# Attention of chunks 4 to 23 with plain float32 score products on both row halves, in place of split q and k

## The chip, the cores and the metric

The kernel runs on one core of one Trainium2 chip. The metric is device time in microseconds (us) of one execution, as a median of several runs; lower is better. Engines are named as in the profile: PE is TensorE (PEld its weight loads), DVE is VectorE, ACT is ScalarE, POOL is GpSimd, SP is SyncE, which issues most transfers.

## The reference

Three parts follow one another, for 4 batches of 768 tokens (3072 tokens in all) and a model width of 512.

```
# 1. retention: 8 heads of width 64, decay gamma per head
state = gamma * state + k_t (outer) v_t
y_t   = scale * q_t @ state                       # q, k, v: (4, 8, 768, 64)
# 2. gated block, per token
xn = y / sqrt(mean(y*y) + 1e-6) * rms_g
x2 = (silu(xn @ w_gate) * (xn @ w_val)) @ w_out   # 512 -> 1536 -> 512
# 3. second block, per token
h = x2 @ w_in                                     # 512 -> 1024
u = h * softmax(h)
out = layernorm(u) * g_ln @ w_out2                # 1024 -> 512
```

The weights arrive as 64-bit floats. All results are wanted in float32 accuracy.

## The kernel before

**Precision.** The two feed-forward blocks use a fast float32 format (F32R in the code) whose operands carry fewer bits, so each operand is split in a high and a low part (`split`, L89: ACT copies the high part, DVE or POOL subtracts it). Each product then is three matmuls of 512 columns (`mm3`, L563: high·high, high·low, low·high, lines L564 to L566). Plain float32 matmuls appear in a trace as two records each.

**Tiling.** The tokens are worked on in six blocks of 512 (`NB`), each of four chunks of 128 tokens (`NCB`), 24 chunks in all; six chunks make a batch (`CPB`), at whose first chunk the retention state starts afresh (no product with the state) and at whose last none is kept. Within a chunk the recurrence is a small attention: scores k·q of 128 x 128 per head, times a decay mask (`mtab_t`), times v; plus the product of the decayed q (`qd`) with the state `U`; then `U` is decayed and the chunk's k·v (`kd`, decayed k) is added. A pair of heads (index p, halves hh) shares the 128 partitions: each head has 64 rows.

**Stages.** Chunks 0 to 3 are done in a prologue (`first_scores` and its neighbours). Then `bc_block(n)` runs the gated block of token block n: 12 steps (m), each with two groups of products into the PSUM banks GB and VB and one (`cmm`) into four banks X. `de_block(n)` runs the second block. Block 0's second block is held back and run after block 1's. While block n is being multiplied, the attention of block n+1 is fed in between: `att_pieces(n + 1)` returns a list of small functions that are spread over numbered slots (`span` slots; 30 for the attention of block 1, 45 for block 2, 35 for later ones), followed by the steps of the root-mean-square norm (`rms_steps`). In blocks 0 and 1 the weights are converted from 64-bit as well (`conv_a`, `conv_g`, `conv_b`, `w_split`, `w2_fin`): block 0 converts the gated block's weights and stores them split in DRAM, block 1 converts those of the second block (keys "in" and "out", 16 pieces). `conv_g` writes a sign tile: into the PSUM bank YB once the prologue is over, into the SBUF tile `sq` before that.

**Order of the work.** The tile framework orders the instructions of every engine by a simulated schedule with program order as priority; each engine and each transfer queue then works strictly in that order.

**Banks.** Of the eight PSUM banks, SB and YB serve attention. For each chunk before the change there are two units u of four heads, each with pieces a, b, c:
- Block 1 (chunks 4 to 7): `att_scores4`, four plain float32 products per unit on that unit's half of the rows (L195), one mask on DVE (L197).
- Blocks 2 to 5 (chunks 8 to 23): `att_prep` splits k and q (ACT L117 and L119, DVE L118 and L120): high k in one half of the rows and low k in the other, q high and q low side by side in 256 columns. `att_scores` then makes two heads' scores by two matmuls of 256 columns (L142); ACT copies the low-q half out (L146), DVE adds it (L148) and multiplies the mask (L149).
- `att_av` makes state·q (L159, full array) and A·v (L162, each head 64 columns of the array, so two heads stand side by side); `att_state` makes kd·v (L173, 64 columns too).

Of the kernel before, what the change touches and what calls it, by code (L numbers as in the profile page):

```python
# [35 lines left out]
ONE = (1, 2)  # L36
# [4 lines left out]
def retention_moe_kernel(ctx: ExitStack, tc: tile.TileContext, qk0, q2, kt, kv, wpk, w2i, w2o,  # L41
# [52 lines left out]
    raw, rawk = {}, {}  # L94

    def att_load(gc, u):
        tq = wt("rq", [P, 4, P], F32, 2)
        nc.sync.dma_start(tq, q2[gc, u])
        if u == 0:
            rawk[gc] = wt("rk", [P, 4, P], F32, 1)  # L100
            nc.sync.dma_start(rawk[gc], kt[gc])
        tv = wt("rv", [P, 512], F32, 2)
        nc.sync.dma_start(tv, kv[gc, u])
        raw[gc, u] = (tq, tv)

    prepd = {}

    def att_prep(gc, u, native=False):
        tq, tv = raw.pop((gc, u))
        tk = rawk[gc] if u == 0 else rawk.pop(gc)  # L110
        a, b = slice(64 * u, 64 * u + 64), slice(64 - 64 * u, 128 - 64 * u)
        if native:
            kst, qhl = tk[a], tq[a]
        else:
            kst = wt("kst", [P, 4, P], F32R, 2)
            qhl = wt("qhl", [P, 4, 2, P], F32R, 2)
            nc.scalar.copy(kst[a], tk[a])  # L117
            nc.vector.tensor_tensor(out=kst[b], in0=tk[a], in1=kst[a].bitcast(F32), op=ALU.subtract)  # L118
            nc.scalar.copy(qhl[:, :, 0, :], tq)  # L119
            nc.vector.tensor_tensor(out=qhl[:, :, 1, :], in0=tq, in1=qhl[:, :, 0, :].bitcast(F32), op=ALU.subtract)  # L120
        kd = qd = None
        if gc % CPB != CPB - 1:
            kd = wt("kd", [P, 4, 64], F32, 2)
            nc.gpsimd.tensor_tensor(
                out=kd, in0=tv[:, 0:256].rearrange("p (h d) -> p h d", h=4),
                in1=ktab_t[:, 4 * u:4 * u + 4].unsqueeze(2).to_broadcast([P, 4, 64]), op=ALU.mult)
        if gc % CPB != 0:
            qd = wt("qd", [P, 2, P], F32, 2)
            tq4 = tq.rearrange("p (a b) i -> p a b i", b=2)
            for hh in range(2):  # L130
                r = slice(64 * hh, 64 * hh + 64)
                nc.gpsimd.tensor_tensor(out=qd[r], in0=tq4[r, :, hh, :],  # L132
                                        in1=qtab_t[r, 2 * u:2 * u + 2, :], op=ALU.mult)
        prepd[gc, u] = (kst, qhl, kd, qd, tv)

    scored = {}

    def att_scores(gc, p):
        u, hl = p // 2, 2 * (p % 2)
        kst, qhl, kd, qd, tv = prepd[gc, u]  # L140
        for hh in range(2):
            nc.tensor.matmul(SB[:, hh * 256:hh * 256 + 256], lhsT=kst[:, hl + hh, :],  # L142
                             rhs=qhl[:, hl + hh].rearrange("p s i -> p (s i)"), start=True, stop=True)
        s4 = SB.rearrange("p (h s i) -> p h s i", h=2, s=2)
        s2 = wt("s2", [P, 2, P], F32, 1)
        nc.scalar.copy(s2, s4[:, :, 1, :])  # L146
        A = wt("A", [P, 2, P], F32, 2)
        nc.vector.tensor_tensor(out=A, in0=s4[:, :, 0, :], in1=s2, op=ALU.add)  # L148
        nc.vector.tensor_tensor(out=A, in0=A, in1=mtab_t[:, 2 * p:2 * p + 2, :], op=ALU.mult)  # L149
        scored[gc, p] = A  # L150

    def att_av(gc, p, Y=YB, at=0):
        u = p // 2
        kst, qhl, kd, qd, tv = prepd[gc, u]
        A = scored.pop((gc, p))
        cs = slice((p - at) * P, (p - at) * P + P)
        first = gc % CPB == 0
        if not first:
            nc.tensor.matmul(Y[:, cs], lhsT=U[gc % 2][:, p, :], rhs=qd[:, p % 2, :], start=True, stop=False)  # L159
        for hh in range(2):  # L160
            hl = 2 * (p % 2) + hh
            nc.tensor.matmul(Y[64 * hh:64 * hh + 64, cs], lhsT=tv[:, 256 + 64 * hl:320 + 64 * hl],  # L162
                             rhs=A[:, hh, :], start=first, stop=True)

    def att_state(gc, u, S=SB, at=0):
        if gc % CPB == CPB - 1:
            return
        kst, qhl, kd, qd, tv = prepd[gc, u]
        sv = S[:, at:at + 128].rearrange("p (a e) -> p a e", a=2)
        for pl in range(2):  # L170
            for hh in range(2):
                hl = 2 * pl + hh
                nc.tensor.matmul(sv[64 * hh:64 * hh + 64, pl, :], lhsT=kd[:, hl, :],  # L173
                                 rhs=tv[:, 256 + 64 * hl:320 + 64 * hl], start=True, stop=True)
        for hh in range(2):
            r = slice(64 * hh, 64 * hh + 64)
            ps = slice(2 * u, 2 * u + 2)
            state_update(gc, r, ps, sv[r])

    def state_update(gc, r, ps, sv):  # L180

        old, new = U[gc % 2][r, ps, r], U[(gc + 1) % 2][r, ps, r]
        if gc % CPB == 0:
            nc.vector.tensor_copy(new, sv)
        else:
            nc.gpsimd.tensor_tensor(out=new, in0=old,
                                    in1=utab_t[r, ps].unsqueeze(2).to_broadcast([64, ps.stop - ps.start, 64]),
                                    op=ALU.mult)
            nc.vector.tensor_tensor(out=new, in0=new, in1=sv, op=ALU.add)

    def att_scores4(gc, u, S=SB):

        kst, qhl, kd, qd, tv = prepd[gc, u]
        for hl in range(4):
            nc.tensor.matmul(S[:, hl * P:hl * P + P], lhsT=kst[:, hl, :], rhs=qhl[:, hl, :], start=True, stop=True)  # L195
        A = wt("r2", [P, 4, P], F32, 8)
        nc.vector.tensor_tensor(out=A, in0=S.rearrange("p (h i) -> p h i", h=4),  # L197
                                in1=mtab_t[:, 4 * u:4 * u + 4, :], op=ALU.mult)
        for pl in range(2):
            scored[gc, 2 * u + pl] = A[:, 2 * pl:2 * pl + 2, :]  # L200

    def att_y(gc, Y=YB):
# [7 lines left out]

    def att_yu(gc, u, Y):

        c = gc % NCB
        cs = slice(c * P, c * P + P)
        nc.scalar.copy(xT[:, 2 * u:2 * u + 2, cs], Y[:, 0:256].rearrange("p (a i) -> p a i", a=2))
        if u:
            sq = f4()[:, 0, :].rearrange("p (a i) -> p a i", a=4)
            nc.scalar.activation(sq, xT[:, :, cs], AF.Square)
            nc.vector.tensor_reduce(out=ssq[:, cs], in_=sq.rearrange("p a i -> p i a"), axis=AX.X, op=ALU.add)
# [95 lines left out]
    def first_scores(c, banks, halves=(0, 1)):  # L315

        for hh in halves:
            r = slice(64 * hh, 64 * hh + 64)
# [650 lines left out]
```

## Time and profile before

| | |
|---|---|
| median of 3 runs | 1041.49 us (1039.58, 1043.09, 1041.49) |
| the profiled execution | 1040.31 us, span 1038.5 us from its first to its last instruction |
| granted TensorE clock, mean | 0.995 of full speed |
| PE busy | 1014.7 us (98% of the span), 5174 matmul records |
| DVE, ACT, POOL busy | 542.5, 412.5, 329.5 us (52%, 40%, 32%) |

Busy times are unions of the intervals in which an engine's records run. Matmuls are pipelined and overlap, so what a matmul costs is read from the distance between the starts of its neighbours, not from its own duration.

### The profile page before, as it was taken

What the parts mean: (1) busy time and instruction counts of PE and PEld (TensorE: products, weight loads), DVE (VectorE), ACT (ScalarE), POOL (GpSimd) and SP (SyncE); (2) the same over time, 40 slices, a digit from 0 to 9 for tenths busy, and PEclk for the clock granted to TensorE, in tenths of its full rate; (3) what the DMA queues carried; (4) which work ended last, traced back from release to release, by engine and by line L of the source; (5) the groups of instructions that cost most, each with busy time, mean ns of one, the idle gap of its engine ahead of it and who ended that gap; (6) DMA issues with size and microseconds to landing.
All of it is one profiled execution on the core that took longest, in us unless ns stands there. A gap on an engine that the chain in (4) does not pass through costs nothing.

```text
span 1038.5 us, 14176 instructions
## 1 busy us (share of the span) xinstructions
PE 1014.7 (98%) x5174; PEld 817.8 (79%) x5174; DVE 542.5 (52%) x1014; ACT 412.5 (40%) x785; POOL 329.5 (32%) x414
## 2 busy tenths in 40 slices
PE   9899998998999999999999999999999999999998
PEld 7777876777888887878777877878787877888887
DVE  5887776787466733344681444483445366111162
ACT  3667655564345442222462322343223325211243
POOL 6876863675124221121251011142111015000031
PEclk9999998999999999999999999999999999999999
DMA  9699997796622015666403666510665510455301
GB/s 345 212 335 389 346 353 267 268 335 229 198 82 62 21 51 173 209 211 198 132 21 102 195 223 220 183 31 31 214 196 201 189 62 21 142 187 198 102 1 41
DMA packets 60485, 181.10 MB, mean 174 GB/s; under 512 B 7168, under 2 KB 7552, under 8 KB 60416
## 3 DMA queue, kind: packets, MB, share of 16 engines
q1 hardware_dynamic: 51632, 155.03, 44.6%
q10 hardware_dynamic: 8784, 25.17, 6.1%
q8 instruction: 41, 0.67, 0.3%
q14 instruction: 28, 0.23, 0.1%
HBM read 153.96 MB, written 26.21 MB: 173 GB/s over the span
## 4 chain that ended last, share of the span: by engine, by line
PE 80%; DVE 8%; issue 4%; POOL 4%; ACT 2%; DMA 1%; SPq 0%; ACTq 0%; POOLq 0%; DVEq 0%
PE X L565 11%; PE X L566 11%; PE X L564 11%; PE GB L564 7%; PE GB L566 7%; PE GB L565 7%; PE VB L564 6%; PE VB L566 6%; PE VB L565 6%; POOL st L470 2%; DVE st L469 1%; PE YB L162 1%; PE SB L142 1%; PE YB L159 1%; DVE st L482 1%
## 5 line engine op out<-in xcount | busy, mean ns | idle before, releaser
L581 DVE TENSOR_TENSOR f<-VB,f 128x512 f32<-128x512 f32 x72 | 49.6, 689 | 165.8 <-PE VB L566 156.9
L132 POOL TENSOR_TENSOR qd<-rq,qtab_t 64x256 f32<-64x256 f32 x68 | 56.3, 828 | 224.4 <-PE YB L159 145.7
L564 PE MATMUL GB<-xnh,w 128*128 128x512 f32 (+1 forms) x268 | 105.5, 394 | 1.2 <-ACT w L90 0.9
L564 PE MATMUL VB<-xnh,w 128*128 128x512 f32 (+1 forms) x268 | 106.0, 396 | 0.0
L565 PE MATMUL GB<-xnl,w 128*128 128x512 f32 (+1 forms) x268 | 104.7, 391 | 0.8 <-DVE xnl L286 0.8
L565 PE MATMUL X<-r,wo 128*128 128x512 f32 x264 | 104.3, 395 | 1.1 <-DVE r L91 1.1
L566 PE MATMUL GB<-xnh,w 128*128 128x512 f32 (+1 forms) x268 | 104.2, 389 | 0.3 <-DVE w L91 0.3
L566 PE MATMUL VB<-xnh,w 128*128 128x512 f32 (+1 forms) x268 | 104.2, 389 | 0.0
L565 PE MATMUL VB<-xnl,w 128*128 128x512 f32 (+1 forms) x268 | 103.8, 387 | 0.0
L566 PE MATMUL X<-r,wo 128*128 128x512 f32 x264 | 103.6, 392 | 0.0
L564 PE MATMUL X<-r,wo 128*128 128x512 f32 x264 | 98.2, 397 | 0.8 <-ACT r L90 0.8
L609 ACT ACTIVATE f<-GB 128x512 f32<-128x512 f32 x72 | 42.9, 596 | 134.8 <-PE GB L566 131.0
L90 ACT CAST r<-f 128x512 fp32r<-128x512 f32 x72 | 44.6, 619 | 113.3 <-DVE f L581 113.0
L470 POOL TENSOR_TENSOR st<-st,x 128x512 int32<-128x512 int32 x52 | 70.1, 1350 | 41.8 <-ACT x L467 14.1
L91 DVE TENSOR_TENSOR r<-f,r 128x512 fp32r<-128x512 f32 x72 | 59.6, 827 | 32.3 <-ACT r L90 32.0
L148 DVE TENSOR_TENSOR A<-SB,s 128x256 f32<-128x256 f32 x64 | 27.0, 422 | 91.4 <-ACT s L146 90.8
L681 POOL TENSOR_TENSOR sm<-sm 128x1 f32<-128x1 f32 x24 | 5.4, 225 | 201.2 <-DVE sm L659 170.3
L146 ACT COPY s<-SB 128x256 f32<-128x256 f32 x64 | 23.9, 374 | 98.6 <-PE SB L142 98.6
L564 PEld LDWEIGHTS GB<-xnh,w 128*128 128x128 f32 x268 | 50.5, 188 | 12.6 <-ACT w L90 1.4
L565 PEld LDWEIGHTS GB<-xnl,w 128*128 128x128 f32 x268 | 50.5, 188 | 11.4 <-DVE xnl L286 1.2
L564 PEld LDWEIGHTS VB<-xnh,w 128*128 128x128 f32 x268 | 50.5, 188 | 11.0 <-issue 1.2
L565 PEld LDWEIGHTS X<-r,wo 128*128 128x128 f32 x264 | 49.6, 188 | 11.9 <-DVE r L91 1.6
(241 smaller groups left out, 2358.1 us busy)
## 6 DMA issues: line engine op xcount, KB each, us to landing
w<-scr SPq DMA_DIRECT2D x120, 512.0 KB, 3.4
wo<-scr SPq DMA_DIRECT2D x60, 512.0 KB, 3.4
x<-in_wpk SPq DMA_DIRECT2D x36, 512.0 KB, 6.3
rq<-in_q SPq DMA_DIRECT2D x40, 256.0 KB, 3.5
rv<-in_kv SPq DMA_DIRECT2D x40, 256.0 KB, 3.5
scr<-CV ACTq DMA_DIRECT2D x18, 512.0 KB, 6.5
scr<-w ACTq DMA_DIRECT2D x12, 512.0 KB, 6.3
out<-f ACTq DMA_DIRECT2D x23, 256.0 KB, 2.0
```

Of the source, the lines that this page charges most:

```text
L90: nc.scalar.copy(hi, src)
L91: (lo_eng or nc.vector).tensor_tensor(out=lo, in0=src, in1=hi.bitcast(F32), op=ALU.subtract)
L132: nc.gpsimd.tensor_tensor(out=qd[r], in0=tq4[r, :, hh, :], in1=qtab_t[r, 2 * u:2 * u + 2, :], op=ALU.mult)
L142: nc.tensor.matmul(SB[:, hh * 256:hh * 256 + 256], lhsT=kst[:, hl + hh, :], rhs=qhl[:, hl + hh].rearrange("p s i -> p (s i)"), start=True, ...
L146: nc.scalar.copy(s2, s4[:, :, 1, :])
L148: nc.vector.tensor_tensor(out=A, in0=s4[:, :, 0, :], in1=s2, op=ALU.add)
L470: nc.gpsimd.tensor_tensor(out=ti, in0=ti, in1=lo, op=ALU.add)
L564: nc.tensor.matmul(ps, lhsT=lh, rhs=rh, start=start, stop=False)
L565: nc.tensor.matmul(ps, lhsT=lh, rhs=rl, start=False, stop=False)
L566: nc.tensor.matmul(ps, lhsT=ll, rhs=rh, start=False, stop=stop)
L581: nc.vector.tensor_tensor(out=a, in0=GV[1], in1=silu[:, 0, :], op=ALU.mult)
L609: nc.scalar.activation(s[:, 0, :], GV[0], AF.Silu)
```

## The change

The split of q and k goes. For chunks 4 to 23 a chunk is now one unit of eight heads. `att_load` brings q and k in pairs of heads (first head of a pair in rows 0 to 63, second in rows 64 to 127), by eight transfers of 64 KB, and k and v in one of 512 KB. `att_scores` makes plain float32 products of 128 columns, pair after pair and within a pair first the upper then the lower half of the rows, into SB and YB; each bank then gets one mask instruction (`att_mask`, 128x512). The pieces per chunk are: a (scores of all eight heads), b (state product, then preparation of the next chunk), c (state·q and A·v of all four pairs, evaluation, load of the chunk after the next). For block 1, where YB is in use by the conversion, the two halves' scores are separate pieces a0 and a1 through SB, then c, then d (state). `kd` and `qd` are one POOL instruction each per chunk. `conv_g` uses the SBUF tile `sq` for the 16 pieces of the second block's weights. `first_scores` of the prologue takes the two halves in turn too. At the start two whole chunks are loaded and one prepared, instead of two units and one.

```diff
-    def att_prep(gc, u, native=False):
...
-            kst = wt("kst", [P, 4, P], F32R, 2)
-            qhl = wt("qhl", [P, 4, 2, P], F32R, 2)
-            nc.scalar.copy(kst[a], tk[a])
-            nc.vector.tensor_tensor(out=kst[b], in0=tk[a], in1=kst[a].bitcast(F32), op=ALU.subtract)
-            nc.scalar.copy(qhl[:, :, 0, :], tq)
-            nc.vector.tensor_tensor(out=qhl[:, :, 1, :], in0=tq, in1=qhl[:, :, 0, :].bitcast(F32), op=ALU.subtract)
...
+    def att_load(gc):
+        tq, tk = wt("rq", [P, 4, P], F32, 2), wt("rk", [P, 4, P], F32, 2)
+        tv = wt("rv", [P, 2, 512], F32, 2)
+        for t, src in ((tk, lambda u: kt[gc, 64 * u:64 * u + 64]), (tq, lambda u: q2[gc, u, 0:64])):
+            for u in range(2):
+                heads = src(u).rearrange("d (a b i) -> d a b i", a=2, b=2)
+                for hh in range(2):
+                    nc.sync.dma_start(t[64 * hh:64 * hh + 64, 2 * u:2 * u + 2, :], heads[:, :, hh, :])
+        nc.sync.dma_start(tv, kv[gc].rearrange("u p x -> p u x"))
...
+    def att_mask(gc, hh, S):
+        A = wt("A", [P, 4, P], F32, 2)
+        nc.vector.tensor_tensor(out=A, in0=S.rearrange("p (a i) -> p a i", a=4), in1=mtab_t[:, hh::2, :], op=ALU.mult)
+        masked[gc, hh] = A
+
+    def att_scores(gc, halves, banks):
+        tq, tk = prepd[gc][0:2]
+        for p in range(4):
+            for hh in halves:
+                r = slice(64 * hh, 64 * hh + 64)
+                nc.tensor.matmul(banks[hh][:, p * P:p * P + P], lhsT=tk[r, p, :], rhs=tq[r, p, :],
+                                 start=True, stop=True)
+        for hh in halves:
+            att_mask(gc, hh, banks[hh])
...
+    def att_av(gc, Y):
...
+        for p in range(4):
+            cs = slice(p * P, p * P + P)
+            if not first:
+                nc.tensor.matmul(Y[:, cs], lhsT=U[gc % 2][:, p, :], rhs=qd[:, p, :], start=True, stop=False)
             for hh in range(2):
...
+                nc.tensor.matmul(Y[64 * hh:64 * hh + 64, cs], lhsT=att_v(tv, p, hh), rhs=A[hh][:, p, :],
+                                 start=first, stop=True)
...
     def first_scores(c, banks, halves=(0, 1)):
-        for hh in halves:
-            r = slice(64 * hh, 64 * hh + 64)
-            for p in range(4):
+        for p in range(4):
+            for hh in halves:
+                r = slice(64 * hh, 64 * hh + 64)
...
+            def a(gc=gc):
+                att_scores(gc, (0, 1), (SB, YB))
+            def a0(gc=gc):
+                att_scores(gc, (0,), (SB, SB))
+            def a1(gc=gc, nxt=nxt):
+                att_scores(gc, (1,), (SB, SB))
                 if nxt:
+                    att_prep(nxt)
+            def b(gc=gc, nxt=nxt):
+                att_state(gc, SB)
+                if nxt:
+                    att_prep(nxt)
+            def c(gc=gc, nx2=nx2, Y=SB if n == 1 else YB):
+                att_av(gc, Y)
+                att_y(gc, Y)
+                if nx2 and n > 1:
+                    att_load(nx2)
+            def d(gc=gc, nx2=nx2):
+                att_state(gc, SB)
                 if nx2:
+                    att_load(nx2)
+            out += [a0, a1, c, d] if n == 1 else [a, b, c]
...
     def conv_g(key):
-        g = YB if begun[0] else wt("sq", [P, 512], F32, 1)
+        g = YB if begun[0] and key[0] not in ("in", "out") else wt("sq", [P, 512], F32, 1)
...
-    att_load(NCB, 0)
-    att_load(NCB, 1)
-    att_prep(NCB, 0, native=True)
+    att_load(NCB)
+    att_load(NCB + 1)
+    att_prep(NCB)
```

## Rows read from the trace of the kernel before

**Rows 1.** The page, busy time by engine: us, share of span, instructions.

```profile
PE 1014.7 (98%) x5174; PEld 817.8 (79%) x5174; DVE 542.5 (52%) x1014; ACT 412.5 (40%) x785; POOL 329.5 (32%) x414
```

**Rows 2.** Stretches: length, busy PE, PEld, DVE, ACT, POOL (instructions), PEclk, DMA, GB/s.

```profile
34.00:60.00 26.00, 23.05 (x148) 18.12 (x146) 21.33 (x29) 14.46 (x25) 23.18 (x24) 1.00 0.64 200
...
150.00:166.00 16.00, 11.87 (x51) 8.35 (x51) 11.71 (x16) 10.22 (x18) 12.75 (x12) 0.94 0.98 373
166.00:172.00 6.00, 6.00 (x17) 4.84 (x18) 5.46 (x9) 4.77 (x9) 0.38 (x1) 0.59 0.73 260
172.00:289.00 117.00, 112.68 (x571) 90.30 (x570) 73.96 (x115) 56.64 (x104) 57.17 (x54) 1.00 0.73 248
...
383.00:505.00 122.00, 122.00 (x629) 97.44 (x628) 50.97 (x88) 36.03 (x68) 20.65 (x35) 1.00 0.59 195
505.00:526.00 21.00, 19.01 (x100) 15.03 (x99) 15.63 (x40) 8.57 (x20) 6.23 (x11) 1.00 0.16 46
526.00:532.00 6.00, 6.00 (x24) 4.83 (x23) 4.68 (x14) 1.82 (x5) 6.00 (x6) 0.72 0.01 3
...
690.00:698.00 8.00, 5.95 (x35) 4.78 (x33) 7.26 (x16) 7.40 (x17) 6.11 (x8) 1.00 0.00 0
```

**Rows 3.** Timeline of PE around a score pair and one A·v block.

```profile
423.86 0.40 PE L142 MATMUL SB<-qhl,kst 128*128 128x256 f32 x2
424.09 0.39 PE L566 MATMUL GB<-xnh,w 128*128 128x512 f32 x1
424.41 0.44 PE L162 MATMUL YB<-A,rv 128*64 128x128 f32 x4
...
425.12 0.39 PE L565 MATMUL GB<-xnl,w 128*128 128x512 f32 x1
425.35 0.39 PE L566 MATMUL GB<-xnh,w 128*128 128x512 f32 x1
```

**Rows 4.** Timeline of PE around a state product joined to an A·v.

```profile
429.25 0.39 PE L564 MATMUL X<-r,wo 128*128 128x512 f32 x1
429.57 0.45 PE L173 MATMUL SB<-rv,kd 128*64 128x64 f32 x8
429.85 0.39 PE L162 MATMUL YB<-A,rv 128*64 128x128 f32 x4
...
430.51 0.39 PE L566 MATMUL X<-r,wo 128*128 128x512 f32 x1
```

**Rows 5.** Timeline of PE around four plain float32 scores on one row half.

```profile
67.81 0.39 PE L565 MATMUL GB<-xnl,CV 128*128 128x512 f32 x1
68.13 1.16 PE L195 MATMUL SB<-rq,rk 64*128 64x128 f32 x8
...
69.55 0.39 PE L565 MATMUL VB<-xnl,CV 128*128 128x512 f32 x1
```

**Rows 6.** Timeline of PE, the prologue's scores of one chunk, one half after the other.

```profile
12.82 1.71 PE L320 MATMUL X<-QK 64*128 64x128 f32 x16
```

**Rows 7.** The conversion's last step (L482) by operand: ns min/median/max, first to last start.

```profile
L482 DVE SCALAR_TENSOR_TENSOR st<-st,YB x45: 670/676/690, 57.5 to 247.1; 128x512 f32<-128x512 f32 x45
...
L482 DVE SCALAR_TENSOR_TENSOR st<-st,sq x7: 673/683/1779, 21.8 to 53.6; 128x512 f32<-128x512 f32 x7
```

**Rows 8.** Groups on DVE, 165 to 289 us: busy us, mean ns | idle before.

```profile
L149 DVE TENSOR_TENSOR A<-A,mtab_t 128x256 f32<-128x256 f32 x12 | 8.8, 732 | 0.2
...
L120 DVE TENSOR_TENSOR qhl<-rq,qhl 128x512 fp32r<-128x512 f32 x6 | 5.5, 920 | 0.1
L118 DVE TENSOR_TENSOR kst<-rk,kst 64x512 fp32r<-64x512 f32 x6 | 5.2, 864 | 1.8 <-ACT kst L117 1.6
L148 DVE TENSOR_TENSOR A<-SB,s 128x256 f32<-128x256 f32 x12 | 5.0, 420 | 13.5 <-ACT s L146 13.4
```

**Rows 9.** The chain that ended last, 159 to 168 us: start, us, what.

```profile
160.32 0.68 DVE kst L118
...
163.54 0.69 DVE qhl L120
```

More of the change, by code (lines that the diff above doesn't have):

```diff
@@ L127, in att_prep @@
         if gc % CPB != 0:
-            qd = wt("qd", [P, 2, P], F32, 2)
-            tq4 = tq.rearrange("p (a b) i -> p a b i", b=2)
-            for hh in range(2):
-                r = slice(64 * hh, 64 * hh + 64)
[L132 to L163, printed above, removed]
@@ new lines, in att_v @@
+    def att_v(tv, p, hh):
+        h = 2 * p + hh
+        return tv[:, h // 4, 256 + 64 * (h % 4):320 + 64 * (h % 4)]
+    def att_av(gc, Y):
+        tq, tk, tv, kd, qd = prepd[gc]
+        first = gc % CPB == 0
+        A = [masked.pop((gc, hh)) for hh in range(2)]
+        for p in range(4):
+            cs = slice(p * P, p * P + P)
+            if not first:
+                nc.tensor.matmul(Y[:, cs], lhsT=U[gc % 2][:, p, :], rhs=qd[:, p, :], start=True, stop=False)
+            for hh in range(2):
+                nc.tensor.matmul(Y[64 * hh:64 * hh + 64, cs], lhsT=att_v(tv, p, hh), rhs=A[hh][:, p, :],
+                                 start=first, stop=True)
@@ L166, in att_state @@
+    def att_state(gc, S):
         if gc % CPB == CPB - 1:
             return
-        kst, qhl, kd, qd, tv = prepd[gc, u]
-        sv = S[:, at:at + 128].rearrange("p (a e) -> p a e", a=2)
-        for pl in range(2):
+        tq, tk, tv, kd, qd = prepd[gc]
+        sv = S[:, 0:256].rearrange("p (a e) -> p a e", a=4)
+        for p in range(4):
             for hh in range(2):
-                hl = 2 * pl + hh
-                nc.tensor.matmul(sv[64 * hh:64 * hh + 64, pl, :], lhsT=kd[:, hl, :],
-                                 rhs=tv[:, 256 + 64 * hl:320 + 64 * hl], start=True, stop=True)
+                h = 2 * p + hh
+                nc.tensor.matmul(sv[64 * hh:64 * hh + 64, p, :], lhsT=kd[:, h // 4, h % 4, :], rhs=att_v(tv, p, hh),
+                                 start=True, stop=True)
@@ L175, in att_state @@
         for hh in range(2):
             r = slice(64 * hh, 64 * hh + 64)
[L177 to L200, printed above, removed]
@@ L202, in att_y @@
-    def att_y(gc, Y=YB):
+            old, new = U[gc % 2][r, :, r], U[(gc + 1) % 2][r, :, r]
+            if gc % CPB == 0:
+                nc.vector.tensor_copy(new, sv[r])
+            else:
+                nc.gpsimd.tensor_tensor(out=new, in0=old, in1=utab_t[r].unsqueeze(2).to_broadcast([64, 4, 64]),
+                                        op=ALU.mult)
+                nc.vector.tensor_tensor(out=new, in0=new, in1=sv[r], op=ALU.add)
+    def att_y(gc, Y):
         c = gc % NCB
@@ new lines, in att_pieces @@
+        for gc in range(NCB * n, NCB * n + NCB):
+            nxt = gc + 1 if gc + 1 < NB * NCB else None
+            nx2 = gc + 2 if gc + 2 < NB * NCB else None
+            def a(gc=gc):
[4 more added lines that the diff above has]
+                att_scores(gc, (1,), (SB, SB))
+                if nxt:
+                    att_prep(nxt)
[10 more added lines that the diff above has]
+                att_state(gc, SB)
@@ L421, in c @@
                 if nx2:
-                    att_load(*nx2)
-            out += [a, b, c]
+                    att_load(nx2)
+            out += [a0, a1, c, d] if n == 1 else [a, b, c]
         return out
```

75 lines of the change are left out of this document (11 added, 64 removed).

## The prediction

> **What bounds the kernel now.** The page's first part comes first: PE runs 1014.7 of 1038.5 us, the next engine little over half [rows 1]. So what PE does in sequence is the time, and two things can change it: the length of PE's own work, and its gaps. The table of stretches says where the gaps are [rows 2]. From 383 to 505 us, where only attention and the first block run, PE is busy 122.00 of 122.00 us: whatever DVE and ACT save there is worth nothing, and whatever PE gets more is paid in full. Gaps stand in a few places: 2.95 us at 34 to 60, 4.1 at 150 to 166 (edge from block 0 to block 1), 4.3 at 172 to 289 (block 1, with the second conversion and attention of block 2), 2.0 at 505 to 526 (edge to block 3), 2.05 at 690 to 698. After two of them the granted clock drops: 0.59 on average over 166 to 172 and 0.72 over 526 to 532, which with levels of 1.2 and 2.4 GHz means 4.9 and 3.4 us at the lower one and half of that, 2.5 and 1.7 us, lost. After the gap at 690 it stays at 1.00 [rows 2].
>
> **What PE pays for attention.** Starts of neighbours give prices. An ordinary product takes 0.23 us (425.12 to 425.35), and a pair of heads' scores of split operands the same (423.86 to 424.09): 0.92 us a chunk [rows 3]. An A·v block in the middle of ordinary products costs far more than its work. From 424.09 to 425.12 is 1.03 us; less the two ordinary products in it, 0.57. Its four records run two by two (in 0.44 us with ends), 0.11 us each step, so 0.35 us is the price of going to 64-column halves and back [rows 3]. State and A·v together take 1.26 - 0.46 = 0.80 us, thus one such price, 0.22 for A·v and 0.23 for four state products [rows 4]. Four plain scores on one half of the rows take 1.74 - 0.46 = 1.28 us: eight records at 0.11 are 0.89, the way in and out 0.39 [rows 5].
>
> **The change on PE.** New scores of a chunk are sixteen records. If the halves overlap they take 0.89 + 0.39 = 1.28 us against 0.92. That they can overlap is seen in the prologue: eight on one half took 1.16 us [rows 5], so sixteen in a row would take 1.16 + 8 x 0.11 = 2.04; they took 1.71 though the second half is queued behind the whole first half [rows 6]. I take full overlap; without it a chunk costs 0.89 more.
> State is now a block of its own, 0.35 + 0.46 = 0.81; before, its two parts shared blocks with A·v and cost 0.23 each. A·v keeps four blocks a chunk, since state·q on the full array stands between the pairs in piece c; state·q itself is as often and as long. An ordinary chunk of blocks 2 to 5 thus goes from 0.92 + 2 x 0.57 + 2 x 0.80 = 3.66 to 1.28 + 0.81 + 4 x 0.57 = 4.37, +0.71 us; there are eleven. Chunks 11, 17 and 23 have no state: +0.36 each. Chunks 12 and 18 have no state·q, so the eight A·v share one block (0.35 + 0.88): 3.66 to 3.32, -0.34 each. Sum 7.8 + 1.1 - 0.7 = +8.2. In block 1 scores stay at two blocks of 1.28; chunks 4 and 7 give +0.35 each for the state's own block, 5 and 6 come out even: +0.7. Together +8.9 us, of which 25 more blocks are 25 x 0.35 = 8.8. Pieces that the schedule cuts in two pay the price again; I add 1.0 (three cuts), bounds 0 and 7 (one in each of 20 chunks).
> What the price consists of matters here. The row shows 0.09 us between the end of the ordinary step (424.09 + 0.23) and 424.41; the rest of 0.35 is weight loading that no longer hides and the way back [rows 3]. The Trainium skill (TensorEngine Tiling, Key Properties) says that changing the tiling mode drains the array, and speaks against a change with more changes of mode. Were the drain all, 25 blocks would cost 25 x 2 x 0.09 = 4.5 us instead of 8.8; I stay with the row.
>
> **What other engines lose, and what that frees.** For each unit ACT drops L117, L119 and two L146; DVE drops L118, L120 and two each of L148, L149. In 165 to 289 us these are 8.8 + 5.5 + 5.2 + 5.0 = 24.5 us of DVE [rows 8]. Eight masks of 128x512 with one operand in PSUM come in at some 0.68 (L482 in that form [rows 7]): 5.5 us. Against that, `conv_g` moves: the 16 conversions now read the sign tile from SBUF. With YB such an instruction takes 670 to 690 ns; with `sq` between 673 and 1779 [rows 7]. I take the middle of that range less 0.68, 0.55 each, 8.8 us (0 to 17.6). DVE in block 1 is left with 10.2 us less; in 172 to 289 it had 74 [rows 2].
> The gaps one by one. At 150 to 166 the chain runs through kst (0.68) and qhl (0.69) on DVE and a second kst between them, all ahead of what PE waits for [rows 9]: I take 2.6 of 4.1, and 2.5 for the clock, since a rest of 1.5 us is shorter than the gap at 690 that cost no clock. At 172 to 289 I take 4.0 of 4.3: A·v of block 2 waits for masks behind kst and qhl, and in the new order A is ready a whole piece before. At 505 to 526 DVE is busy 15.6 of 21 us with kst and qhl among it [rows 2]: 1.8 of 2.0, and 1.7 of clock. At 34 to 60 POOL is busy 23.2 of 26 us [rows 2], and preparation falls there from six instructions to two larger ones: 1.0 of 2.95. The gap at 690 I leave. In the prologue the interleaved scores are shorter by up to 0.55 us a chunk, mostly beside loads: 0.4 (0 to 2.2). Sum: 2.6 + 2.5 + 4.0 + 1.8 + 1.7 + 1.0 + 0.4 = 14.0; bounds 4 (only the prologue's and half of block 1's, the clock falls anyway) and 19.3 (all of it).
>
> **At no cost.** Nine transfers a chunk for five, with 1.02 MB for 1.28: each is asked for a whole chunk before its use, and DMA is at 0.59 in 383 to 505 [rows 2]. In block 0, where it stands at 0.98 around 150 us, small pieces could cost what the bytes save; without cover 0.5 MB of them at twice the time is 1.4 us a chunk at 373 GB/s, 5.6 in four. SP issues more, and weight loads queue behind; they have several slots in hand. Piece b waits on PE for the mask of SB, and c for that of YB; the pieces lie three slots apart and ordinary products fill them; if DVE is late, the next `cmm` is what waits. Fewer POOL instructions for kd and qd are idle time of an engine that seldom decides.
>
> **Sum.** 1040.31 + 8.9 + 1.0 - 14.0 = 1036.2 for an execution like the profiled one, which lies 1.2 us under the median of the runs; so 1037.4 as a median.
>
> **Rivals.** A measurement of this kernel tells 0.3%, 3.1 us, from no change: faster means below 1038.4, slower above 1044.6.
> First, the gaps shrink about as much as PE's work grows: relief of 7 to 12.5 us instead of 14.0, some 1041. For it: a schedule that is laid out anew often opens gaps elsewhere, and DVE at 690 is held up by the norm, not by attention.
> Second, the sign tile in SBUF keeps DVE the bottleneck of block 1: the conversion starts at the edge at 150 to 166 and lasts through block 1, so 2.6 + 2.5 + 4.0 = 9.1 us of relief hang on it: 1037.4 + 9.1 = 1046.5, slower. It decides when the 16 instructions take near 1.7 us each, so that 17.6 of the 19 us saved are gone. Against it: the median of the seven was 683 ns [rows 7]. The Trainium skill (SBUF — State Buffer, SBUF: two separate sides) says that a DVE instruction with two SBUF inputs and a GpSimd instruction lock each other out for a whole instruction; the 670 to 690 with YB and the 1779 with `sq` agree.
> Third, the halves of the rows do not overlap: 16 chunks x 0.89 = 14.2 more, 1051.6. The 1.71 us speak against it [rows 6].
> Fourth, everything is freed and no piece is cut: 1041.5 + 8.9 - 19.3 = 1031.1.
>
> **How the numbers follow.** Forecast with its neighbourhood up to the fourth case: 0.47 faster (0.37 and 0.10). First rival 0.29. Second 0.19, third 0.05. So faster 0.47, same 0.29, slower 0.24. The likeliest alone spans 1033 to 1038.4 or so; the range of 8 in 10 goes from 1030 to 1048, as it takes in the second rival and the fourth case and leaves out the third.
>
> **What would show it.** Right: score records of two halves that start within a few ns; 0.11 us steps; 1.28 us between the ordinary products around piece a; six blocks in an ordinary chunk; PE still gapless from 383 to 505 but that stretch longer by some 1.8 us (three times 0.71 less 0.34); no low clock after 166 and 526; L482 spread between 0.68 and 1.8. Wrong: gaps of over 2 us at the edges still there, or PE idle at piece a or b for a bank that DVE or ACT still reads, or pieces scattered in more blocks than six.

## The result, and the profile after

The changed kernel takes 1054.1 us in the median (1052.2 to 1055.8), against 1041.6 before: a ratio of 1.0121, 95% interval 1.0097 to 1.0145. That is slower by 12.5 us where 4 us faster was forecast. Of the 85 executions of the kernel before that were taken beside the runs below, 34 take 1049 to 1058 us with a mean granted clock of 0.97 to 0.98, where the others have 0.99 or more and a median of 1040.3 us; differences below are against 1040.3, and the ratios hold some of the former, which widens their intervals.

The page of the changed kernel, busy time by engine (us, share, instructions):

```profile
PE 1028.9 (98%) x5302; PEld 826.0 (79%) x5302; DVE 449.1 (43%) x822; ACT 354.1 (34%) x649; POOL 280.5 (27%) x321
```

The span is 1052.2 us, 13.7 more than before. PE's busy time rose by 14.2 us, while DVE lost 93 us and ACT 58 [rows 1]. PE's idle time is 23.3 us; before, it was 1038.5 - 1014.7 = 23.8. So PE does more, and the relief on the other engines bought no idle time back on balance. Where it went is in the stretches (columns as in [rows 2]; an edge is the passage from one block to the next):

```profile
0.00:34.00 34.00, 25.87 (x238) 20.95 (x238) 16.37 (x31) 12.57 (x28) 18.58 (x26) 0.87 0.83 284
34.00:60.00 26.00, 24.15 (x145) 20.30 (x146) 22.52 (x34) 16.46 (x29) 20.10 (x18) 0.84 0.75 252
...
150.00:164.00 14.00, 14.00 (x82) 11.36 (x81) 8.45 (x14) 7.19 (x13) 8.57 (x8) 1.00 1.02 410
164.00:172.00 8.00, 8.00 (x38) 6.04 (x37) 6.95 (x11) 4.84 (x9) 1.53 (x2) 1.00 0.69 268
172.00:289.00 117.00, 114.12 (x587) 89.49 (x585) 62.06 (x77) 45.70 (x77) 48.76 (x38) 1.00 0.72 243
...
383.00:508.00 125.00, 125.00 (x645) 99.38 (x643) 29.11 (x44) 24.87 (x42) 9.30 (x13) 1.00 0.55 177
...
526.00:532.00 6.00, 4.05 (x27) 3.16 (x26) 5.96 (x14) 1.98 (x4) 1.56 (x6) 0.87 0.19 54
...
690.00:706.00 16.00, 14.05 (x69) 11.09 (x68) 14.25 (x36) 7.18 (x16) 6.64 (x11) 0.89 0.12 34
...
857.00:878.00 21.00, 17.61 (x76) 14.17 (x75) 17.18 (x48) 8.63 (x20) 9.98 (x11) 0.92 0.00 1
```

The opening and the last edge before the change, in the same view:

```profile
0.00:34.00 34.00, 30.90 (x255) 24.71 (x256) 22.06 (x40) 16.35 (x35) 21.85 (x28) 1.00 0.89 322
...
855.00:875.00 20.00, 18.41 (x94) 15.07 (x93) 15.74 (x41) 10.94 (x23) 11.23 (x13) 1.00 0.04 14
```

Against these and [rows 2]: the gap of 4.1 us at 150 to 166 and the low clock behind it are gone, and block 1 idles 2.9 us instead of 4.3. But the gap in front of block 3 (1.95 us at 526 to 532) and that at 690 to 706 are as large as before, the one at 857 to 878 has 3.4 us for 1.6, the clock drops behind all three, and the opening up to 34 us idles 8.1 us for 3.1.

The same view from the first ordinary product (a product of the feed-forward blocks) to the end, the changed kernel first:

```profile
37.49:1052.18 1014.69, 1000.47 (x5055) 802.86 (x5055) 429.23 (x785) 338.09 (x615) 260.04 (x293) 0.99 0.49 163
34.47:1038.52 1004.05, 983.30 (x4918) 792.78 (x4917) 520.00 (x975) 396.09 (x750) 307.25 (x386) 0.99 0.50 169
```

The first product comes 3.0 us later, and the rest takes 10.7 us more. Of these, idle time is -6.5 (14.2 for 20.75). The half clock takes 7.5 us of the busy time (it lasts up to 42.3 us, and for 3.4 us at each of the three edges) where it took 2.5 + 1.7 = 4.2: +3.3. What is left, PE's own work at full clock, is 993.0 for 979.1: +13.9.

A chunk's scores on PE's timeline, in the middle of block 2's attention:

```profile
450.84 0.39 PE L510 MATMUL VB<-xnh,w 128*128 128x512 f32 x1
451.16 0.37 PE L129 MATMUL SB<-rq,rk 64*128 64x128 f32 x1
451.17 0.37 PE L129 MATMUL YB<-rq,rk 64*128 64x128 f32 x1
451.37 0.27 PE L129 MATMUL SB<-rq,rk 64*128 64x128 f32 x1
451.38 0.27 PE L129 MATMUL YB<-rq,rk 64*128 64x128 f32 x1
451.48 0.27 PE L129 MATMUL SB<-rq,rk 64*128 64x128 f32 x1
...
452.25 0.50 PE L508 MATMUL X<-r,wo 128*128 128x512 f32 x1
```

The halves overlap: records come in pairs 6 to 7 ns apart, one of each half, in steps of 0.11 us after a first of 0.21. From 450.84 + 0.23 to 452.25 is 1.18 us where 1.28 was reckoned. What was not reckoned stands a little earlier:

```profile
389.45 0.39 PE L510 MATMUL GB<-xnh,w 128*128 128x512 f32 x1
389.77 0.43 PE L147 MATMUL YB<-A,rv 128*64 128x128 f32 x2
390.13 0.48 PE L129 MATMUL SB<-rq,rk 64*128 64x128 f32 x2
390.55 0.50 PE L508 MATMUL X<-w2oh,r 128*128 128x512 f32 x1
390.89 0.40 PE L509 MATMUL X<-w2ol,r 128*128 128x512 f32 x1
391.21 0.48 PE L129 MATMUL SB<-rq,rk 64*128 64x128 f32 x2
391.63 0.50 PE L510 MATMUL X<-w2oh,r 128*128 128x512 f32 x1
```

A plain float32 product leaves two records. So this is one product of A and v, one score, two ordinary products and again one score: the schedule has drawn products of several pieces ahead, one at a time. Each pays the way off the full array and back: from 389.45 + 0.23 to 390.55, 0.87 us for two products of 0.22; from 390.89 + 0.23 to 391.63, 0.51 for one. Call a group a run of neighbouring records on one division of the array (half its rows or half its columns), and count from 45 us on: there were 87 before and are 135 now, 48 more where 25 were reckoned.

The theory after the result: the loss is the number of groups, at 0.35 us each as in [rows 3]; beside it stand an opening delayed by small transfers, and gaps at the edges that have another cause than the attention's work on DVE. The rivals: grouping costs nothing (drawn-ahead products fill waits), or one cause carries it all.

### The profile page after: what moved, and what is told of

Its sections match the earlier page's. It is cut to its first block, busy times and chain, and to the rows that moved or that the text cites. A ratio compares the mean times of both kernels' runs of the same rounds, so it can differ in the third digit from the quotient of the medians.

```text
span 1052.2 us, 13974 instructions
## 1 busy us (share of the span) xinstructions
PE 1028.9 (98%) x5302; PEld 826.0 (79%) x5302; DVE 449.1 (43%) x822; ACT 354.1 (34%) x649; POOL 280.5 (27%) x321
## 4 chain that ended last, share of the span: by engine, by line
PE 89%; DVE 6%; DMA 3%; POOL 1%; issue 1%; ACT 1%; SPq 0%; POOLq 0%; ACTq 0%; DVEq 0%
PE X L508 11%; PE X L510 11%; PE X L509 11%; PE GB L508 8%; PE GB L509 8%; PE GB L510 8%; PE VB L508 7%; PE VB L510 7%; PE VB L509 7%; PE YB L147 2%; PE SB L129 2%; PE YB L145 2%; DVE st L426 2%; PE X L616 1%; PE SB L158 1%; DMA x<-in_wpk 1%
## 5 line engine op out<-in xcount | busy, mean ns | idle before, releaser
L90 DVE TENSOR_TENSOR r<-f,r 128x512 fp32r<-128x512 f32 x72 | 54.8, 762 | 36.3 <-ACT r L89 35.8
L166 POOL TENSOR_TENSOR U<-U,utab_t 64x256 f32<-64x256 f32 x26 | 18.4, 707 | 191.6 <-PE YB L145 190.1
L508 PEld LDWEIGHTS VB<-xnh,w 128*128 128x128 f32 x268 | 50.4, 188 | 15.4 <-DVE f L525 3.7
L508 PEld LDWEIGHTS GB<-xnh,w 128*128 128x128 f32 x268 | 50.8, 190 | 11.2 <-ACT xnh L240 0.5
L509 PEld LDWEIGHTS GB<-xnl,w 128*128 128x128 f32 x268 | 50.8, 190 | 10.7 <-DVE xnl L244 0.8
L510 PEld LDWEIGHTS GB<-xnh,w 128*128 128x128 f32 x268 | 50.8, 189 | 10.1
L510 PEld LDWEIGHTS VB<-xnh,w 128*128 128x128 f32 x268 | 50.4, 188 | 10.5 <-issue 0.2
L509 PEld LDWEIGHTS VB<-xnl,w 128*128 128x128 f32 x268 | 50.4, 188 | 9.8
```

Of the source, the lines that this page charges most:

```text
L90: (lo_eng or nc.vector).tensor_tensor(out=lo, in0=src, in1=hi.bitcast(F32), op=ALU.subtract)
L508: nc.tensor.matmul(ps, lhsT=lh, rhs=rh, start=start, stop=False)
L509: nc.tensor.matmul(ps, lhsT=lh, rhs=rl, start=False, stop=False)
L510: nc.tensor.matmul(ps, lhsT=ll, rhs=rh, start=False, stop=stop)
```

## Experiments

### The number of groups

`uncut`: the attention's products are queued behind the last ordinary product traced before them.

```diff
+    lastmm = [None]
...
+    def behind():
+        return tc.issue_after(lastmm[0].ins) if lastmm[0] else nullcontext()
...
-        nc.tensor.matmul(ps, lhsT=ll, rhs=rh, start=False, stop=stop)
+        lastmm[0] = nc.tensor.matmul(ps, lhsT=ll, rhs=rh, start=False, stop=stop)
...
-                att_av(gc, Y)
+                with behind():
+                    att_av(gc, Y)
```

The same stands around the scores and the state's products.

> The attention's products of chunks 4 to 23 may no longer be drawn ahead of the last ordinary product traced before them, so that a group of a piece stays together in TensorE's order; the built order then has 118 groups of products off the full array after the first ordinary product, against 137 in the changed kernel. Theory (a group of products off the full array costs about 0.36 us, and the change made 48 more such groups, not 25): 19 groups fewer, -7 us, 1047 us. Rival A (a drawn-ahead product filled a wait, so that keeping the groups together only brings the waits back): 1054 us with the waits on TensorE up by 7 us. Rival B (the loss lies in the small transfers at the start and in the low clock, not in the groups): 1054 us.

`ufirst`: the four state products of a chunk ahead of its eight products of A and v.

```diff
+        for p in range(0 if first else 4):
+            cs = slice(p * P, p * P + P)
+            nc.tensor.matmul(Y[:, cs], lhsT=U[gc % 2][:, p, :], rhs=qd[:, p, :], start=p == 0, stop=False)
         for p in range(4):
             cs = slice(p * P, p * P + P)
-            if not first:
-                nc.tensor.matmul(Y[:, cs], lhsT=U[gc % 2][:, p, :], rhs=qd[:, p, :], start=True, stop=False)
             for hh in range(2):
...
-                                 start=first, stop=True)
+                                 start=first, stop=first or p == 3)
```

> In piece c the four state products (full array) are issued first and the eight products of A and v behind them, in one group instead of four; the work is the same. The built order has 89 groups off the full array, against 137 in the changed kernel. Theory (a group costs about 0.36 us): 48 groups fewer, -17 us, 1037 us. Rival A (the products of A and v cost what they cost, however they are grouped): 1054 us. Rival B (the small transfers at the start and the low clock carry the loss): 1054 us, all of TensorE's records off the ordinary products unchanged in sum.

`both`: the two edits together.

> Both edits together, the groups kept whole and the state products first: 67 groups off the full array against 137. Theory: 70 fewer at 0.36 us, -25 us, 1029 us. Rival A: waits come back for the drawn-ahead products, some 1035 to 1040 us. Rival B: 1054 us.

`merge`: as `both`, and in blocks 2 to 5 the state's products move from piece b to behind A·v in piece c (the edit against `both`).

```diff
             def b(gc=gc, nxt=nxt):
-                with behind():
-                    att_state(gc, SB)
...
                 with behind():
                     att_av(gc, Y)
+                    if Y is YB:
+                        att_state(gc, SB)
```

> As before it, and in blocks 2 to 5 the products of the state's update stand directly behind those of A and v, so that a chunk has two groups off the full array: 54 in all against 137. Theory: 83 fewer at 0.36 us, -30 us, 1024 us, if nothing waits for the later state. Rival A: the state comes too late for the next chunk and TensorE waits some 0.5 us for it in each of 16 chunks, 1030 us or more. Rival B: 1054 us.

Measured (groups counted in the records after 45 us; the changed kernel and the four made from it have the same 5302 records on PE):

| kernel | median us | ratio to before, interval | groups | PE busy us |
|---|---|---|---|---|
| before | 1040.3 | | 87 | 1014.7 |
| changed | 1054.1 | 1.0121 (1.0097 to 1.0145) | 135 | 1028.9 |
| uncut | 1048.0 | 1.0055 (1.0021 to 1.0090) | 117 | 1024.0 |
| ufirst | 1039.3 | 0.9967 (0.9933 to 1.0001) | 87 | 1012.9 |
| both | 1031.8 | 0.9909 (0.9879 to 0.9938) | 66 | 1002.4 |
| merge | 1025.3 | 0.9854 (0.9806 to 0.9902) | 53 | 995.3 |

The times lie within 3 us of what the theory gave. By the medians a group costs (1054.1 - 1025.3) / 82 = 0.35 us, by the busy time (1028.9 - 995.3) / 82 = 0.41. The clock doesn't carry this: PE's work behind the first ordinary product, without idle time and with the half clock taken out as above, falls from 993.0 to 962.1 us, 0.37 a group. The first rival falls: less than 5 us of waits came back (idle 27.8 us in `merge`, 23.3 in the changed kernel). With before's 87 groups (`ufirst`) the change is worth 1 us, which cannot be told from nothing. One chunk of `ufirst` on PE's timeline:

```profile
465.19 0.39 PE L511 MATMUL VB<-xnh,w 128*128 128x512 f32 x1
465.41 1.05 PE L144 MATMUL YB<-qd,U 128*128 128x128 f32 x8
466.40 1.09 PE L148 MATMUL YB<-A,rv 128*64 128x128 f32 x16
467.42 0.50 PE L509 MATMUL X<-r,wo 128*128 128x512 f32 x1
```

State·q and A·v of a whole chunk take 2.0 us here, from 465.42 to 467.42; in four groups of 0.57 [rows 3] A·v alone took 2.3. The Trainium skill (TensorEngine Tiling, Key Properties) says that a change of the tiling mode drains the array. The ranking by groups agrees; the 0.09 us that [rows 3] show on the way in, taken for both ways, would be 0.18 a group, and 0.35 was measured.

### The opening

On the changed kernel's timeline of SP, ACT and PE, nine transfers for chunk 4 and then chunk 5's stand in SP's order, the latter around a load of weights (x):

```profile
15.57 4.48 SPq L102 DMA_DIRECT2D rk<-in_kt  x4
20.09 4.28 SPq L102 DMA_DIRECT2D rq<-in_q  x4
24.41 0.59 SPq L103 DMA_DIRECT2D rv<-in_kv  x1
25.05 3.29 SPq L102 DMA_DIRECT2D rk<-in_kt  x4
28.38 0.61 SPq L102 DMA_DIRECT2D rq<-in_q  x1
29.12 0.50 SPq L389 DMA_DIRECT2D x<-in_wpk  x1
...
25.21 1.13 ACT L207 ACTIVATE xT<-YB,rg_t 128x128 f32<-128x128 f32 x4
...
31.26 0.75 ACT L411 ACTIVATE x<-x,two 128x512 f32<-128x512 uint32 x1 [4.93 <-DMA rk<-in_kt]
...
34.14 2.08 PE L710 MATMUL SB<-f,ones 128*128 128x128 f32 x8 [4.71 <-ACT f L205]
```

ACT idles 4.9 us ahead of L411, and the work for the next chunk's norm (L205) is queued behind it; PE waits 4.7 us for that, and runs at half clock from 32.1 to 42.3 us. The first ordinary product comes at 37.5 us, before at 34.5.

It is not the weights that ACT waits for, though the expectations below take it so. The piece of x that L411 reads (by the semaphore that it waits for, 104 in the trace) was issued at 14.29 us and had landed at 23.82. The chain that ended last, 22 to 38 us (start, us, what), names what released ACT:

```profile
26.27 4.52 DMA rk<-in_kt
...
30.82 0.02 ACTq L457
...
30.87 0.34 ACTq L457
31.26 0.75 ACT x L411
```

L457 is ACT's own store of converted weights (scr<-w), which stands ahead of L411 in ACT's order. In the trace it carries the same semaphore (108) as a transfer of chunk 5's k that was issued at 26.27, and it waits until that one has landed, at 30.80. So an engine that reads nothing of chunk 5 stands behind one of its transfers. The runs below move or merge these transfers, and both ways of the delay, a late load of weights and a store behind a transfer, would go with that; it is the trace that tells them apart.

`start1`: the second chunk's `att_load` moves from the start into block 1's first piece.

> The loads of the second chunk after the opening (chunk 5: eight transfers of 64 KB and one of 512 KB) are issued in the first piece of block 1's attention instead of at the start. Theory (the first ordinary product is late because SP issues these transfers in front of a load of expert weights, and TensorE idles 5.0 us at 29.1 us and runs at half clock behind it): the first product comes at 35 us instead of 37.5, the whole takes 3 us less, 1051 us. Rival (the load that is late would be late anyway, for the first chunk's eight transfers or for the queue's bytes): 1054 us with the first product at 37.5 us.

1054.7 us, ratio 1.0086 (1.0040 to 1.0133): nothing. The schedule put the transfers into the same place of SP's order, so the run tells of neither. `start3` queues them behind a later load on SP:

```diff
-        nc.sync.dma_start(t, src)
+        lastx[0] = nc.sync.dma_start(t, src)
...
+                if gc == NCB:
+                    with tc.issue_after(lastx[0].ins):
+                        att_load(nxt)
...
-    att_load(NCB + 1)
```

> The loads of chunk 5 (eight of 64 KB, one of 512 KB) are held on SP behind later loads of expert weights, so that SP's order has them eight places later. (The earlier edit start1 left SP's order as it was, so it tested nothing.) Theory (these transfers stand in front of the weights for which ScalarE, and behind it TensorE, waits 5.0 us at 29.1 us): the weight load is issued some 7 us sooner, at 25 us or before, the wait falls to under 1 us as in the kernel before, first ordinary product near 34.5 us against 37.5, -3 us, 1051 us. Rival (the wait stays because the first chunk's eight transfers alone hold SP up to 24 us): 1053 to 1054 us.

1053.2 us, ratio 1.0134 (1.0099 to 1.0169). The first ordinary product came at 34.4 us, as the theory said, and the end did not follow: the chunk was late in its turn. PE waited 1.4 us up to 79 us, and 1.8 us up to 169, the edge to block 1, and by the 480th ordinary product the kernel was 4.5 us behind the changed one.

`bigload`: q and k of a chunk side by side in the input.

```diff
...
-                for hh in range(2):
-                    nc.sync.dma_start(t[64 * hh:64 * hh + 64, 2 * u:2 * u + 2, :], heads[:, :, hh, :])
...
+        t = wt("rqk", [P, 2, 4, P], F32, 2)
...
+        nc.sync.dma_start(t, q2[gc])
```

> q and k of a chunk lie side by side in the input, as the array's rows take them, so that a chunk's loads are two transfers of 512 KB instead of eight of 64 KB and one of 512 KB; nothing else changes. Theory (at the start the small transfers take SP 0.55 us each in front of the weights' load; behind the start they are hidden): the first ordinary product comes at 34.5 to 35 us against 37.5, -3 us, 1051 us. Rival (small transfers are dear all along, 160 of them): -6 us or more, 1048 us. Rival (they cost nothing): 1054 us.

1048.3 us, ratio 1.0084 (1.0062 to 1.0105). SP of `bigload` over the same time:

```profile
15.99 0.33 SPq L98 DMA_DIRECT2D rqk<-in_q  x1
17.27 0.38 SPq L100 DMA_DIRECT2D rv<-in_kv  x1
...
21.99 11.42 SPq L386 DMA_DIRECT2D x<-in_wpk  x4
```

Chunk 4's loads hold SP for 1.7 us instead of 9.4 (some 4 us of these are waits until earlier transfers have landed), and the next load of weights is issued at 22.0 us instead of 29.1. The first ordinary product comes at 33.0 us, and the 4.5 us are kept: 4.8 at the 480th, 7.4 at the end of the profiled execution. The gain by the medians is 5.9 us, which is the size of the rival (small transfers dear all along) and not of the theory. The trace bears out the place that the theory named: behind the first product PE idles 14.2 us in both kernels, and of the other 2.9 us 2.7 are the clock, which is at half for a shorter time in the opening and does not drop behind the gap in front of block 3.

`scorder`: the opening's scores in before's order, one half and then the other.

> The opening chunks' scores go back to the order of the kernel before, one half of the rows and then the other. Theory (the opening's order is no part of the loss: the scores only end sooner in front of the same wait for the values): 1054 us, the first ordinary product at 37.5 us. Rival (the interleaved scores bring the idle time of 2 us at 6 us and the low clock behind it, which is passed on): the clock stays high from 8 us on, first product 1 to 2 us earlier, 1052 us.

1052.1 us, ratio 1.0099 (1.0047 to 1.0151), from 1048.2 to 1063.0. The clock did stay high up to 33 us in its profiled execution, but the first ordinary product came at 38.7 us, later. This does not decide between the two.

### The edges

VectorE of the changed kernel in front of block 3, and PE's first product after the gap:

```profile
521.29 2.74 DVE L197 SCALAR_TENSOR_TENSOR xT<-xT,rg_t,ssq 128x512 f32<-128x512 f32 x4
...
525.89 2.49 DVE L90 TENSOR_TENSOR xnl<-xT,xnh 128x512 fp32r<-128x512 f32 x4
...
528.89 0.68 DVE L90 TENSOR_TENSOR r<-GB,r 128x512 fp32r<-128x512 f32 x1
...
529.63 0.50 PE L508 MATMUL GB<-w2oh,r 128*128 128x512 f32 x1 [1.95 <-DVE r L90]
```

PE waits for the split `r` of the transposed tile, and the next block's norm (L197, L90 on xnl) stands 5.2 us long in front of it, though the first product of block 3 that reads it starts at 540.82 us. In the kernel before, DVE's order at this edge was another:

```profile
511.65 1.11 DVE L118 TENSOR_TENSOR kst<-rk,kst 64x512 fp32r<-64x512 f32 x1
...
513.39 0.69 DVE L120 TENSOR_TENSOR qhl<-rq,qhl 128x512 fp32r<-128x512 f32 x1
...
524.12 0.67 DVE L91 TENSOR_TENSOR r<-GB,r 128x512 fp32r<-128x512 f32 x1
...
530.48 3.09 DVE L239 SCALAR_TENSOR_TENSOR xT<-xT,rg_t,ssq 128x512 f32<-128x512 f32 x4
```

There kst and qhl stood ahead of the splits, and the same norm step (L239) behind them.

`edge` gave later slots to the four norm steps.

> In blocks 2 to 4 the last four steps of the norm for the next block (four products with the norm's factors and four splits on VectorE) are placed in slots 46 to 50 of the block, not 41 to 47, behind the splits of the transposed tile. Theory (the waits of 2.2, 2.2 and 3.7 us at 527, 697 and 868 us are for splits on VectorE that stand behind the norm's work, which has moved into the place of the attention's): the three waits shrink to under 1 us each and the low clock behind them goes: -5 to -8 us, 1047 to 1049 us. Rival (the norm is then late for the next block's first products, and TensorE waits there as long): 1054 us or more.

1054.5 us, ratio 1.0123 (1.0091 to 1.0156), the same three waits: the schedule kept VectorE's order, and the run tells nothing. `edge4` queues the steps behind the splits:

```diff
+            lo_ins = split(hi, lo, bank)
+        trlo[0] = lo_ins
...
+        def late(k):
+            with tc.issue_after(trlo[0].ins):
+                rms_3(ssq, k)
```

> In blocks 2 to 4 the four norm steps for the next block are held on VectorE behind the splits of the block's first transposed tile. (The earlier edit edge left VectorE's order as it was and tested nothing.) Theory (the waits of 2.2, 2.2 and 3.7 us at 527, 697 and 868 us are for these splits, which stand behind five microseconds of the norm's work on VectorE): the three waits fall to under 1 us each, and the half clock behind them goes, -6 to -10 us, 1044 to 1048 us. Rival A (the splits wait for other work as long, the maxima of the next tile or the masks): under 2 us gained. Rival B (the norm is late for the next block): slower than 1054 us.

1042.5 us, ratio 1.0029 (1.0018 to 1.0041): 11.6 us gained by the medians, more than expected. The stretches of `edge4`:

```profile
526.00:532.00 6.00, 6.00 (x41) 4.52 (x40) 4.95 (x15) 3.15 (x7) 2.60 (x5) 1.00 0.00 0
690.00:706.00 16.00, 16.00 (x86) 12.78 (x85) 13.17 (x33) 9.46 (x20) 7.73 (x13) 1.00 0.16 49
857.00:878.00 21.00, 21.00 (x106) 17.42 (x105) 16.21 (x41) 11.62 (x26) 9.35 (x13) 1.00 0.04 14
```

No gap and no low clock are left at the three edges. Of the 10.2 us between the two profiled executions, 6.8 are idle time behind the first ordinary product, 2.3 the half clock, 0.4 the opening, and 0.7 PE's own work. `beforeedge` puts the same edit into the kernel before.

> The kernel before with the norm steps of blocks 2 to 4 held behind the splits of the first transposed tile, as in edge4. Theory (the gaps at the edges were there before the change for the same reason, 2.5, 2.4 and 1.9 us of waits at 508 to 535, 690 to 706 and 857 to 880 us, and half clock behind one): -5 to -8 us, 1034 us. Rival (before the change the attention's work on VectorE made them): 1040 us or more, the gaps stay.

Counted as the 1040.3 us are, it takes 1034.5 to 1038.3 us (median 1036.5 of five); the ratio over all is 0.9954 (0.9886 to 1.0021). So some 4 us are the norm's place in the kernel before too, a little less than expected, but not at all three edges. In the kernel before, PE waits 1.8 us for a split at 698 us and 1.1 at 864, and with the edit neither wait is there (read from an execution of 1050.0 us). The two waits at block 3's edge, 0.8 and 0.9 us, stay as they were: the norm did not make them, and the rival (the attention's work) is left standing for that edge.

### The sign tile

`sqbefore`: the kernel before with only this line of the change.

```diff
-        g = YB if begun[0] else wt("sq", [P, 512], F32, 1)
+        g = YB if begun[0] and key[0] not in ("in", "out") else wt("sq", [P, 512], F32, 1)
```

> The kernel before with one line of the change alone: the sign tile of the second expert's weight conversion lies in SBUF and not in PSUM. Theory (the place of this tile costs little once VectorE has room and nothing in the kernel before either, beyond a few tenths on each conversion): 1041 us, within 2 us of the kernel before. Rival (the second rival of the prediction: VectorE's conversions in block 1 become slower and the wait for them longer): 1045 to 1047 us.

Counted in the same way it takes 1045.6 to 1047.6 us, in the median 6.8 more than before, and by its profile this is lost between 210 and 260 us, in block 1, where the step takes 1198 ns in the mean for 682: the rival was right. `sqafter`: the changed kernel with that line undone, and block 2's attention kept off YB.

> The changed kernel with the sign tile of the second expert's conversion back in PSUM; the attention traced in block 1 then leaves that bank alone, with its scores in one bank half by half as in the block before. Theory (the attention's relief of VectorE has covered the price of the tile in SBUF, 6.8 us in the kernel before): at most the 3.2 us that TensorE still waits in block 1 are to be had, 1051 to 1055 us. Rival (the second rival of the prediction: the tile's place costs the changed kernel as much as it costs the kernel before): 1047 to 1048 us.

1052.8 us, ratio 1.0047 (0.9998 to 1.0095). The conversion's last step on DVE, 165 to 289 us (busy us, mean ns | idle before), in the changed kernel:

```profile
L426 DVE SCALAR_TENSOR_TENSOR st<-st,sq 128x512 f32<-128x512 f32 x15 | 21.6, 1438 | 10.2 <-POOL st L414 10.2
```

The step takes 1438 ns with the tile in SBUF, some 680 with it in PSUM [rows 7]. The Trainium skill (SBUF — State Buffer, SBUF: two separate sides) says that a DVE instruction with two SBUF inputs and a GpSimd instruction that reads SBUF lock each other out, and that the one that started first keeps the other waiting. The trace agrees: of these 15, the four in front of which no POOL instruction had started take 680 to 683 ns, and the eleven that met a running one take 1428 to 1781. In the changed kernel the relief of DVE covers most of it: in `sqafter` PE is busy for the whole of 172 to 289 us, so that the 2.9 us of idle time go, and 1.3 us by the medians show at the end, which cannot be told from nothing.

### All that helped

`b2` is `merge` with `edge4`.

> The version with two groups a chunk (merge) with the norm steps of blocks 2 to 4 held behind the splits as in edge4. Theory: the waits of 2.4, 2.4 and 2.3 us at its edges go, -5 to -7 us against merge, 1018 to 1020 us. Rival: 1025 us, other work stands in front of the splits.

1018.7 us, ratio 0.9800 (0.9779 to 0.9821). `b1` adds `bigload`.

> All that helped, together: two groups a chunk (merge), the norm steps behind the splits (edge4), a chunk's loads in two transfers (bigload). Theory (the three losses stand side by side, so that their parts add up): 1019 us less the 6 us that bigload gave alone, 1013 us. Rival (the opening's gain is given back at the edge of block 0, as it was with start3): 1018 us.

1010.4 us, ratio 0.9655 (0.9572 to 0.9738), 30 us under the kernel before and 44 under the changed one. PE is busy 991.6 us of its span of 1007.5.

The parts add up: 1018.7 - 5.9 = 1012.8 was due. The rival, that the opening's gain is given back, falls with large transfers.

## Why the prediction was wrong

The direction was wrong because three terms of the sum were: the relief, the cuts, and the transfers of the opening, which stood at nothing. Forecast was -4.1 us for an execution like the profiled one, and +13.7 came. Of the 17.8 between them the relief behind the opening is 10.4 (13.6 forecast, 3.2 come), PE's work 4.0 (9.9 forecast, 13.9 come), the opening 3.4.

- **Price of a group, 0.35 us: right.** `merge` against the changed kernel gives 0.35 over 82 groups. Scores at 1.28 us a chunk: 1.18 measured. The third rival (no overlap) falls.
- **Cuts, 1.0 us for three: failed.** The schedule made 48 groups more, not 25, so 23 cuts and some 8 us by that price; its own upper bound was 7. That `uncut` wins 6 us back with 18 groups fewer shows that they are paid and don't fill waits. The prediction kept the pieces of the source as units, though products are placed one by one. PE's work is only 4.0 us over its sum; the scores came out lower, and which other terms did is not shown.
- **Relief, 14.0: failed, and by most.** Idle time behind the first ordinary product fell by 6.5 us, and the half clock took 3.3 us more where 4.2 less were forecast. (The upper bound of 19.3 does not come out of its parts, which add up to 19.8; that moves the fourth rival by half a microsecond.)
- **At 150 to 166, 2.6 and 2.5 of clock: right and more.** All 4.1 us and the low clock went. That the relief of DVE did it is not shown: in `merge`, with the same relief, PE waits 2.6 us for ACT at 164 and the clock drops there for 3.4 us. Of 34 to 60, 1.0 was taken and 1.1 came, beside a half clock up to 42.3 us.
- **In block 1, 4.0: 1.4 came.** The sign tile costs 0.76 us an instruction in the changed kernel (0.52 in `sqbefore`), 0.55 was taken. Its mechanism, the second rival, holds: 6.8 us in the kernel before. It was not what made the changed kernel slow.
- **At 505 to 526, 1.8 and 1.7 of clock: none came.** The step read kst and qhl in the stretch as what PE waits for. In the kernel before they stand ahead of the split; when they went, the norm moved from behind the splits into the room, and the split waits for that. The prediction saw the norm at 690 and left that gap alone, but did not carry it to the other edges. The gap at 857 grew by 1.8 us, and two more drops of the clock, each of 3.4 us at half, came behind 690 and 857. `edge4` wins 11.6 us.
- **Opening, -0.4: +3.0.** The nine transfers a chunk were priced at nothing with the cover of several slots, and their case without cover by bytes in block 0. At the start there is no cover, and the wait was one that the prediction did not look for: ACT's own store stands behind the landing of a transfer of chunk 5. `bigload` wins 5.9 us.
- **Balance.** The first rival's sentence, that a schedule laid out anew opens gaps elsewhere, was the right one and was given too small a size.

Not settled: what in the opening makes the clock drop at 8 us. The idle time in front of it does not decide alone: `sqbefore` idles 1.9 us there and keeps the clock up to 35 us, `merge` idles 0.95 and then 0.76 us and drops at 10.4.

## What to carry to other kernels

Where PE is the bound, count its changes between full and divided array in the order that is built, not in the source, and price each by a row; here 82 fewer groups with the same products were worth 29 us. A wait is named by what stands in front of its releaser in that engine's order: taking work away from that engine can let other work move up into its place, as the norm did here. A transfer can cost where nothing reads it yet: here ACT's store stood behind its landing, and what released an engine was read from the chain and not from the tile that it works on.

## What the runs showed of the hardware

At the one place read, passing from half the columns straight to half the rows is cheaper than two ways back to the full array: 0.87 - 0.44 = 0.43 us for both groups at 389.77, 0.51 - 0.22 = 0.29 for the single one at 391.21. In the opening an issue of 64 KB on SP took 0.61 us at 28.38, one of 512 KB 0.59 at 24.41: the number of issues told there, not the bytes. An idle time of 4.7 us in the opening goes with 10.2 us at half clock, one of 2.6 us (`bigload`) with 3.4 us. A gap of 1.95 us at block 3's edge was followed by 3.4 us at half clock in the changed kernel, and by none in `bigload`. A DVE step with two inputs in SBUF took 680 ns alone and up to 1781 when it met a running POOL instruction.
